# Two first layers as seven block products on one core

## The chip, the core and the metric

The kernel runs on one core of one Trainium2 chip. Times are device microseconds of one execution of the whole program. The engines are named as in the profile: PE is TensorE's matmuls, PEld its weight loads, DVE is VectorE, ACT is ScalarE, POOL is GpSimd, SP is SyncE, which issues most DMAs.

## What is computed

An attention with softmaxes over features (q) and over the sequence (k), and behind it a two-layer network with a leaky ReLU:

```python
q_s = softmax(q, axis=-1)          # q, k, v: (8, 8, 576, 64)
k_s = softmax(k, axis=2)
kv = einsum('bhsd,bhse->bhde', k_s, v)
attn = einsum('bhsd,bhde->bhse', q_s, kv)
x = attn.transpose(0, 2, 1, 3).reshape(4608, 512)
h = x @ w_in                       # w_in: (512, 2048)
g = maximum(0.01 * h, h)
out = g @ w_out                    # w_out: (2048, 512), float32 result
```

## The kernel before

Both weight matrices are kept on chip in bf16: `w_in_sb` as 4 blocks of 128 channels (`NB`) by 2048 columns, `w_out_sb` as 16 blocks of 128 rows (`NF`). The attention's result for all 4608 tokens is kept transposed, channels on the partitions, in `xT` (4 blocks by 4608, bf16). The network goes over `xT` in 9 tiles of 512 tokens (`TT`), numbered 0 to 8, the loop at L866. For each tile, the first layer (`layer1`, L560) makes 16 blocks `j` of 128 hidden units by 512 tokens, each the sum of 4 matmuls of 512 columns in one PSUM bank; `leaky` (L570) on ScalarE turns each into bf16 (`gj`, 10 buffers). The second layer (`layer2`, L582) goes over 4 subtiles of 128 tokens (`tsub`), 16 matmuls of 512 columns each; `store` (L575) copies the sum to SBUF, on ScalarE in the middle tiles and on VectorE in tile 8, and issues two DMAs on SP. The last subtile of all is split: 384 columns are copied by ScalarE, the remaining 128 by VectorE, and each part is stored by SP and ScalarE's queue side by side.

PSUM has eight banks of 512 float32 columns: six go round as `psB_pool` (first-layer blocks, attention), two as `psO_pool` (second-layer sums).

The attention of batch b (576 tokens) is made ready while earlier tiles run. The order is written out by hand: `at(t, u, ...)` (L594) hangs functions on a step of tile t, and `run(t, u)` (L599) calls them there. Steps 0 to 15 follow the first-layer blocks; steps 16 to 31 follow every fourth matmul of the second layer, so step 19 ends subtile 0 and step 23 subtile 1. For the last batch, 7, during tile 6: `q_exp` after step 2, and after step 5 `q_back`, which sums, normalizes and has `q_turn` (L547) transpose q by DMA into `qX`; at step 23 `attend_all` (L533) does the 16 matmuls of `cross` and the six copies of `x_keep` on ScalarE into `xT`. Tiles 7 and 8 have no attention beside them. The raw inputs of a batch lie in `raw_pool`, 6 buffers of 2304 float32 a partition.

Of the kernel before, what the change touches and what calls it, by code (L numbers as in the profile page):

```python
# [7 lines left out]

FP32 = mybir.dt.float32
BF16 = mybir.dt.bfloat16  # L10
AF = mybir.ActivationFunctionType
ALU = mybir.AluOpType
AX = mybir.AxisListType
# [7 lines left out]
R = 9  # L21
HL = 4
# [3 lines left out]
def kernel(  # L26
# [9 lines left out]
    nc = tc.nc  # L36
# [3 lines left out]
    B, H, S, D = q.shape  # L40
    C = H * D
    T = B * S
    Cm, F = moe_w_in.shape
    F2, O = moe_w_out.shape
    assert Cm == C and F2 == F and L * R == S and HL * 2 == H

    P = 128
    NB = C // P
    NF = F // P
    TT = 512  # L50
    NT = T // TT
    NTS = TT // P
# [2 lines left out]
    const_pool = ctx.enter_context(tc.tile_pool(name="const", bufs=1))  # L55
    w_pool = ctx.enter_context(tc.tile_pool(name="wts", bufs=1))
    xT_pool = ctx.enter_context(tc.tile_pool(name="xT", bufs=1))
    raw_pool = ctx.enter_context(tc.tile_pool(name="raw", bufs=6))
    ke_pool = ctx.enter_context(tc.tile_pool(name="ke", bufs=2))
    qe_pool = ctx.enter_context(tc.tile_pool(name="qe", bufs=2))  # L60
    mx_pool = ctx.enter_context(tc.tile_pool(name="mx", bufs=1))
    small_pool = ctx.enter_context(tc.tile_pool(name="small", bufs=3))
    qT_pool = ctx.enter_context(tc.tile_pool(name="qT", bufs=2))
    g_pool = ctx.enter_context(tc.tile_pool(name="gsb", bufs=10))
    osb_pool = ctx.enter_context(tc.tile_pool(name="osb", bufs=4))

    psB_pool = ctx.enter_context(tc.tile_pool(name="psB", bufs=6, space=bass.MemoryType.PSUM))
    psO_pool = ctx.enter_context(tc.tile_pool(name="psO", bufs=2, space=bass.MemoryType.PSUM))
    BANK_TAG = "bank2k"
# [20 lines left out]
    R7, RE = slice(0, 7), slice(7, R)  # L90
# [9 lines left out]
    nc.gpsimd.memset(zero, 0.0)  # L100
    ident = const_pool.tile([P, P], BF16)
    make_identity(nc, ident)
    identf = const_pool.tile([P, P], FP32)
    make_identity(nc, identf)
    warm = const_pool.tile([P, 1], BF16)
    nc.scalar.activation(out=warm, in_=ident[:, 0:1], func=AF.Exp)
    gate = const_pool.tile([P, 1], FP32)

    w_in_sb = w_pool.tile([P, NB, F], BF16)
    w_out_sb = w_pool.tile([P, NF, O], BF16)  # L110
    xT = xT_pool.tile([P, NB, T], BF16)


    XH, X8, XE = (slice(0, 7), slice(9, 16)), slice(7, 9), slice(16, 20)
    qe1 = const_pool.tile([P, XE.stop, P], BF16, name="qe1")
    vb2 = [const_pool.tile([P, R, 2, 2, D + 2], BF16, name=f"vb{i}") for i in range(2)]
# [85 lines left out]
    def k_exp(b, hs):  # L202
        nc.scalar.activation(  # L203
            out=st[b]["ke"][:, :, hs].rearrange("p r h d -> p h r d"),
            in_=st[b]["k"][:, hs],
            func=AF.Exp,
        )
# [36 lines left out]
    def q_first(b, rs):  # L244
# [3 lines left out]
        for gg in range(2):  # L248
# [5 lines left out]
            for h in range(2):  # L254
                for r in range(n):
                    nc.scalar.activation(
                        out=st[b]["qe"][:, rs.start + r, 2 * gg + h],
                        in_=st[b]["q"][:, 2 * gg + h, rs.start + r],
                        func=AF.Exp,
                        bias=nmax[:, 2 * gg + h, r : r + 1],  # L260
# [47 lines left out]
    def q_exp(b, rs, hs=ALLH):  # L308
        nc.scalar.activation(  # L309
            out=q_cols(b, rs, hs).rearrange("p r h d -> p h r d"),  # L310
            in_=st[b]["q"][:, hs, rs],
            func=AF.Exp,
        )
# [140 lines left out]
    def q_keep(eng, b, r0, n, gs=slice(0, 4)):  # L454
        o, i = st[b]["qT"][:, gs, r0 : r0 + n], st[b]["ps", r0][:, gs]
        if eng is nc.scalar:
            eng.copy(out=o, in_=i)
        else:
            eng.tensor_copy(out=o, in_=i)
# [65 lines left out]
    def attend_rows(b, rows, engs=(nc.scalar, nc.scalar)):  # L525
        groups = ((0, 1),) if rows.stop - rows.start <= 4 else ((0,), (1,))
        for ggs in groups:
            attend(b, ggs, rows)
        return [
            lambda ggs=ggs, hp=hp: x_keep(engs[hp], b, ggs, rows, hp) for ggs in groups for hp in range(2)  # L530
        ]

    def attend_all(b, *parts):  # L533
        for fn in sum([attend_rows(b, *p) for p in parts], []):
            fn()
# [34 lines left out]
    def leaky(o, ph):  # L570
        nc.scalar.activation(out=o, in_=ph, func=AF.Prelu, alpha=LEAKY_SLOPE)  # L571

    out_r = out.rearrange("(b l r) o -> b r l o", b=B, r=R)

    def store(row0, pout, copy=nc.vector.tensor_copy, os=slice(0, O), issue=(nc.sync, nc.sync)):  # L575
        out_sb = osb_pool.tile([P, O], FP32, name="out_sb")[:, os]
        copy(out=out_sb, in_=pout)  # L577
        for i in range(2):
            b, c = divmod(row0 + i * L, S)
            issue[i].dma_start(out=out_r[b, c // L, :, os], in_=out_sb[i * L : (i + 1) * L])  # L580

    def layer2(pout, g_sb, tsub, j, os=slice(0, O)):  # L582
        nc.tensor.matmul(  # L583
            pout,
            lhsT=g_sb[j // 2][:, j % 2, tsub * P : (tsub + 1) * P],
            rhs=w_out_sb[:, j, os],
            start=(j == 0),
            stop=(j == NF - 1),
        )
# [4 lines left out]
    def at(t, u, *fns):  # L594
        while t > 0 and u >= 32:
            t, u = t + 1, u - 32
        hooks.setdefault((t, u), []).extend(fns)

    def run(t, u):  # L599
        for fn in hooks.pop((t, u), ()):  # L600
            fn()
# [3 lines left out]
    def load_all(b, order="kqv"):  # L605
        for name in order:
            st[b][name] = load(dict(q=q, k=k, v=v)[name], b, f"{name}_raw", [(ALLH, ALLR)])
# [130 lines left out]
    def k_front(b, t, u, v, parts=(ALLH,)):  # L738
        at(t, u, lambda: k_begin(b), lambda: q_begin(b), lambda: k_tree(b, ALLH))
        at(t, v, lambda: k_allmax(b), *[lambda hs=hs: k_sub(nc.vector, b, hs) for hs in parts])  # L740

    def q_front(b, t, u):
        at(t, u, lambda: q_max(b, ALLR), lambda: q_sub(nc.vector, b, ALLR))

    def casts(b, t, u):
        at(t, u, lambda: v_cast(nc.gpsimd, b, 0), lambda: v_cast(nc.gpsimd, b, 1))

    def q_back(b, t, u):
        at(t, u, lambda: q_sum(b, ALLR), lambda: q_norm(b, ALLR), lambda: q_turn(b))
# [13 lines left out]
    for t in range(3, B - 1):  # L763
        b = t + 1
        q_front(b, t - 1, 29)
        at(t, 2, lambda b=b: q_exp(b, ALLR))
        if b + 1 < B:
            k_front(b + 1, t, 1, 8)
            casts(b + 1, t, 6)
            at(t, 17, lambda b=b: k_exp(b + 1, ALLH))  # L770
            at(t, 23, lambda b=b: attend_kv(b))
        else:
            at(t, 23, lambda b=b: attend_all(b, (R7,), (RE,)))
        q_back(b, t, 5)
        if b + 2 < B:
            at(t, 5, lambda b=b: load_all(b + 2))


    def g_tiles():
        return [g_pool.tile([P, 2, TT], BF16, name="gj") for _ in range(NF // 2)]  # L780

    g_sb = g_tiles()
# [18 lines left out]
    def end_act(j, ph, half):  # L801
# [4 lines left out]
    t2 = (  # L806
        lambda: q_transpose(0, 6, 2, psO_pool, "pout"),
        lambda: q_keep(nc.vector, 0, 6, 2),
    )
# [45 lines left out]
    pout = [psO_pool.tile([P, O], FP32, name="pout", tag="pout") for _ in range(2)]  # L855
# [7 lines left out]
    for tsub in range(NTS):  # L863
        store(tsub * P, pout[tsub])

    for t in range(1, NT):  # L866
        g_sb = []
        for j in range(NF):
            ph = psB_pool.tile([P, TT], FP32, name="ph", tag=BANK_TAG)
            layer1(j, ph, t * TT, TT)  # L870
            if j % 2 == 0:
                g_sb.append(g_pool.tile([P, 2, TT], BF16, name="gj"))
            leaky(g_sb[j // 2][:, j % 2], ph)
            run(t, j)
        for tsub in range(NTS):
            row0 = t * TT + tsub * P
            if row0 == T - P:
                for os, copy in ((slice(0, 384), nc.scalar.copy), (slice(384, O), nc.vector.tensor_copy)):
                    po = psB_pool.tile([P, os.stop - os.start], FP32, name="pout2", tag=BANK_TAG)
                    for j in range(NF):  # L880
                        layer2(po, g_sb, tsub, j, os)
                    store(row0, po, copy, os, (nc.sync, nc.scalar))
                break
            po = psO_pool.tile([P, O], FP32, name="pout", tag="pout")
            for j in range(NF):
                layer2(po, g_sb, tsub, j)
                if j == NF - 1:
                    store(row0, po, nc.scalar.copy if t < NT - 1 else nc.vector.tensor_copy)
                if j % 4 == 3:
                    run(t, 16 + 4 * tsub + j // 4)  # L890
    assert not hooks, list(hooks)


# [28 lines left out]
```

## Time and profile before

| | |
|---|---|
| Time, median of 3 runs | 281.05 us (281.03 to 281.23) |
| Span of the profiled execution | 279.3 us; its own time is not listed apart from the three, so the median stands beside it, 1.75 us longer |
| Busy share of the span | PE 97%, PEld 48%, DVE 57%, ACT 57%, POOL 18% |
| Granted TensorE clock, 183 us to the end | 1.00 of full speed |
| Longest shares of the chain that ended last | PE `pout` L583 44%, PE `ph` L562 44% |

The busy time of PE counts overlapping matmuls, whose ends are modelled; distances between starts say more. The chain of waits is followed back from the last instruction; "issue" in it is time in which nothing shows as waited for. In the groups by line the columns are: line, engine, operation, output and inputs with shapes, count, busy us, mean ns of one, idle time before and what ended it. In the timeline each row is a start, a length, engine, line and operation; rows with a count merge several. In the answers on stretches each engine has its busy time with the number of instructions, then the granted clock, the DMA share and GB/s.

### The profile page before, as it was taken

To read this page: it belongs to the slowest core of one execution; us is meant where nothing else is said; L and a number is where in the kernel's file an instruction comes from. 1 tells how busy PE (TensorE), PEld (TensorE's weight loads), DVE (VectorE), ACT (ScalarE), POOL (GpSimd) and SP (SyncE) were. 2 spreads that over 40 slices of the span, in tenths; PEclk is the share of its full clock that TensorE was granted. 3 is DMA by queue.
4 is the path that set the end of the run, shared out by engine and by line. 5 is a ranking of instruction groups with operands and counts; after the bars stand their busy time and mean duration, and the time that the engine had idled before them with its cause. 6 is when DMAs were issued, how large, how long until landed. Compare 5 with 4: busy or idle time off the path is not lost.

```text
span 279.3 us, 4849 instructions
## 1 busy us (share of the span) xinstructions
PE 272.3 (97%) x1927; PEld 133.1 (48%) x1954; DVE 158.4 (57%) x228; ACT 159.6 (57%) x283; POOL 49.5 (18%) x55
## 2 busy tenths in 40 slices
PE   8999999999999999999999999999999999999994
PEld 3488644444444454445444544454444444444443
DVE  3986986999999949957794688543700000000021
ACT  4977573783598458744675458644844464146400
POOL 2957460258003004000400140000000000000000
PEclk9999999999999999999999999999999999999999
DMA  7999999977993696099309930333033300330033
GB/s 253 326 209 325 246 242 306 403 269 200 300 410 139 116 405 227 2 307 361 78 9 311 347 77 2 84 77 75 1 87 75 75 1 2 75 75 0 2 75 75
DMA packets 40006, 46.45 MB, mean 166 GB/s; under 512 B 18736, under 2 KB 23344, under 8 KB 39984
## 3 DMA queue, kind: packets, MB, share of 16 engines
q1 hardware_dynamic: 36320, 41.82, 48.3%
q0 software_dynamic: 3504, 4.20, 8.7%
q8 instruction: 15, 0.25, 0.3%
q10 hardware_dynamic: 160, 0.13, 0.2%
q14 instruction: 7, 0.06, 0.1%
HBM read 36.70 MB, written 9.44 MB: 165 GB/s over the span
## 4 chain that ended last, share of the span: by engine, by line
PE 93%; DVE 3%; DMA 2%; issue 1%; ACT 0%; SPq 0%; ACTq 0%
PE pout L583 44%; PE ph L562 44%; DMA k_raw<-in_k_dram 2%; PE po L476 2%; DVE t L157 1%; PE pokv L338 1%; PE pkv L338 1%; PE pkv L416 0%; DVE k_raw L407 0%; ACT ke L203 0%; ACT gj L571 0%; DVE kmax L157 0%; DVE kd L431 0%; DVE kr L391 0%; PE pokv L476 0%
## 5 line engine op out<-in xcount | busy, mean ns | idle before, releaser
L583 PE MATMUL pout<-w_out_sb,gj 128*128 128x512 bf16 (+2 forms) x574 | 126.3, 373 | 1.2 <-issue 0.3
L562 PE MATMUL ph<-xT,w_in_sb 128*128 128x512 bf16 (+1 forms) x631 | 126.1, 357 | 0.5
L571 ACT ACTIVATE gj<-ph 128x512 bf16<-128x512 f32 x144 | 82.2, 601 | 26.0 <-PE ph L562 25.1
L562 PEld LDWEIGHTS <-w_in_sb 128*128 128x128 bf16 x640 | 62.3, 98 | 62.1 <-issue 0.2
L583 PEld LDWEIGHTS <-gj 128*128 128x128 bf16 x592 | 56.5, 98 | 65.6 <-issue 0.2
L577 ACT COPY out_sb<-pout 128x512 f32<-128x512 f32 (+1 forms) x29 | 16.8, 580 | 68.3 <-PE pout L583 43.1
L577 DVE COPY out_sb<-pout 128x512 f32<-128x512 f32 (+1 forms) x8 | 4.8, 637 | 70.8 <-PE pout L583 70.8
L215 POOL CAST vb<-v_raw 128x1152 bf16<-128x1152 f32 x13 | 21.1, 1650 | 81.4 <-DMA v_raw<-in_v_dram 81.4
L318 DVE TENSOR_REDUCE qsum<-qe 128x36 f32<-128x2304 bf16 (+5 forms) x13 | 20.0, 1542 | 10.5 <-ACT qe L309 10.4
L203 ACT ACTIVATE ke<-k_raw 128x2304 bf16<-128x2304 f32 (+2 forms) x13 | 18.0, 1384 | 8.4 <-DVE k_raw L195 8.0
L325 DVE TENSOR_TENSOR qe<-qe,qrec 128x2304 bf16<-128x2304 bf16 (+5 forms) x13 | 21.5, 1657 | 0.5
L242 DVE TENSOR_REDUCE qmax<-q_raw 128x36 f32<-128x2304 f32 (+5 forms) x13 | 20.0, 1539 | 0.1
L309 ACT ACTIVATE qe<-q_raw 128x2304 bf16<-128x2304 f32 (+5 forms) x13 | 17.1, 1315 | 4.3 <-POOL q_raw L301 3.4
L195 DVE TENSOR_TENSOR k_raw<-k_raw,kall 128x1152 f32<-128x1152 f32 (+2 forms) x10 | 18.0, 1820 | 0.3
L301 POOL TENSOR_TENSOR q_raw<-q_raw,qmax 128x512 f32<-128x512 f32 (+3 forms) x7 | 11.8, 1682 | 20.6 <-DMA q_raw<-in_q_dram 13.8
L499 ACT CAST xT<-po 128x448 bf16<-128x448 f32 (+3 forms) x34 | 14.4, 515 | 1.1 <-PE po L476 1.1
L301 DVE TENSOR_TENSOR q_raw<-q_raw,qmax 128x2304 f32<-128x2304 f32 (+1 forms) x6 | 14.0, 2332 | 0.2
L157 DVE TENSOR_TENSOR t<-t 128x256 f32<-128x256 f32 (+2 forms) x22 | 13.2, 599 | 0.7
L358 DVE RECIPROCAL krec<-pokv 128x2 f32<-128x2 f32 x8 | 1.3, 166 | 21.3 <-PE pokv L476 21.3
L157 DVE TENSOR_TENSOR t<-k_raw 128x512 f32<-128x512 f32 (+1 forms) x11 | 11.2, 1016 | 1.2 <-DMA k_raw<-in_k_dram 1.0
L370 PE MATMUL pout<-zero 128*128 128x512 f32 (+3 forms) x18 | 9.6, 659 | 1.0 <-POOL zero L100 1.0
L338 PEld LDWEIGHTS <-ke 64*64 64x64 bf16 x504 | 5.9, 107 | 3.4 <-issue 3.0
(68 smaller groups left out, 105.3 us busy)
## 6 DMA issues: line engine op xcount, KB each, us to landing
out_dram<-out_sb SPq DMA_DIRECT2D x70, 128.0 KB, 2.6
q_raw<-in_q_dram SPq DMA_DIRECT2D x6, 1152.0 KB, 8.8
v_raw<-in_v_dram SPq DMA_DIRECT2D x6, 1152.0 KB, 11.5
k_raw<-in_k_dram SPq DMA_DIRECT2D x5, 1152.0 KB, 6.2
k_raw<-in_k_dram SPq DMA_DIRECT2D x6, 576.0 KB, 6.1
v_raw<-in_v_dram SPq DMA_DIRECT2D x4, 576.0 KB, 7.6
w_in_sb<-in_moe_w_in_dram POOLq DMA_DIRECT2D x7, 256.0 KB, 7.0
w_out_sb<-in_moe_w_out_dram POOLq DMA_DIRECT2D x6, 256.0 KB, 9.3
```

Source lines behind the costliest of these rows:

```text
L157: nc.vector.tensor_tensor(out=o, in0=i0, in1=i1, op=ALU.max)
L195: eng.tensor_tensor(out=ks, in0=ks, in1=st[b]["kall"][:, hs].unsqueeze(2).to_broadcast([P, n, R, D]), op=ALU.subtract,)
L203: nc.scalar.activation(out=st[b]["ke"][:, :, hs].rearrange("p r h d -> p h r d"), in_=st[b]["k"][:, hs], func=AF.Exp,)
L215: eng.tensor_copy(out=o, in_=i)
L242: nc.vector.tensor_reduce(out=o, in_=st[b]["q"][:, hs, rs], axis=AX.X, op=ALU.max)
L301: eng.tensor_tensor(out=qs, in0=qs, in1=st[b]["qmax", rs.start, hs.start].unsqueeze(3).to_broadcast([P, m, n, D]), op=ALU.subtract,)
L318: nc.vector.reduce_sum(out=qsum, in_=q_cols(b, rs, hs), axis=AX.X)
L325: nc.vector.tensor_tensor(out=qes if out is None else out, in0=qes, in1=st[b]["qrec", rs.start, hs.start].unsqueeze(3).to_broadcast([P, n, ...
L562: nc.tensor.matmul(ph, lhsT=w_in_sb[:, cb, j * P : (j + 1) * P], rhs=xT[:, cb, c0 : c0 + n], start=(cb == 0 and first), stop=(cb == NB - 1 ...
L571: nc.scalar.activation(out=o, in_=ph, func=AF.Prelu, alpha=LEAKY_SLOPE)
L577: copy(out=out_sb, in_=pout)
L583: nc.tensor.matmul(pout, lhsT=g_sb[j // 2][:, j % 2, tsub * P : (tsub + 1) * P], rhs=w_out_sb[:, j, os], start=(j == 0), stop=(j == NF - 1),)
```

## The change

The first layers of tiles 7 and 8 (`TA`, `TB`) are done as one product of 2 x 2 blocks: the rows are the two tiles (`XA`, `XB`), the inner blocks two halves of the 512 channels (`CL`, `CR`), the columns two halves of the 2048 hidden units. Instead of eight block products, seven are made, from sums and differences of the blocks (the scheme of Strassen and Winograd), in groups `i` of 128 columns out of each half.

- `weight_sums` (step 12 of tile 6): four differences of weight blocks, t1 to t4, of 2 x 1024 columns each, on VectorE, and a copy b22 on GpSimd, all as float32r in five of the six `raw_pool` buffers, whose tiles are done with.
- The attention of batch 7 moves from step 23 to step 19 of tile 6.
- `token_sums` (step 22): closes the pools of the attention, opens two new ones in their place, and makes s1 to s4 on VectorE (1024 columns each) and the copy a22 on ScalarE, in float32r.
- `pair_layer1(i)`, i = 0 to 7: seven products of 2 matmuls of 512 columns, two products from the bf16 operands (`xT`, `w_in_sb`), five from the float32r sums. ScalarE copies the first (e1), VectorE combines the others in seven adds to e1 and u4 (tile 7, blocks i and 8 + i) and u3 and c22 (tile 8, the same blocks), ScalarE applies the four `leaky`. The one of u4 is held back until the next group's e1 is copied. Tile 8's blocks go into columns of `xT` that belonged to tiles 0 to 3.
- Between the products stands other TensorE work, 8 matmuls a group: in groups 0 and 1 the last subtile of tile 6, from group 2 on the second layer of tile 7, two blocks `j` a group for all four subtiles, whose sums take both `psO` banks and two of `psB`.
- At the end: the last two groups' share of tile 7's second layer (16 matmuls), its four stores with VectorE's copy, and tile 8's second layer, 4 subtiles of 16 matmuls, with ScalarE's copy and two DMAs on SP. The split of the last subtile is gone.

```diff
-    raw_pool = ctx.enter_context(tc.tile_pool(name="raw", bufs=6))
-    ke_pool = ctx.enter_context(tc.tile_pool(name="ke", bufs=2))
...
+    raw_pool = ctx.enter_context(tc.tile_pool(name="raw", bufs=6))
+    front = ctx.enter_context(ExitStack())
+    ke_pool = front.enter_context(tc.tile_pool(name="ke", bufs=2))
...
-        else:
-            at(t, 23, lambda b=b: attend_all(b, (R7,), (RE,)))
...
+    def subtract(eng, o, a, b):
+        eng.tensor_tensor(out=late[o], in0=a, in1=b, op=ALU.subtract)
+
+    def weight_sums():
+        w = lambda cs, fh: w_in_sb[:, cs, fh * (F // 2) : (fh + 1) * (F // 2)]
+        for n in ("t1", "t3", "t2", "t4", "b22"):
+            late[n] = raw_pool.tile([P, 2, R * HL * D // 2], F32R, name=n, tag="raw")[:, :, 0 : F // 2]
+        subtract(nc.vector, "t1", w(CL, 1), w(CL, 0))
+        subtract(nc.vector, "t2", w(CR, 1), plain("t1"))
+        subtract(nc.vector, "t3", w(CR, 1), w(CL, 1))
+        subtract(nc.vector, "t4", w(CR, 0), plain("t2"))
+        nc.gpsimd.tensor_copy(out=late["b22"], in_=w(CR, 1))
+
+    def token_sums():
+        front.close()
+        pool = ctx.enter_context(tc.tile_pool(name="late", bufs=1, reuse_waits="tile"))
+        late["pool"] = ctx.enter_context(tc.tile_pool(name="late2", bufs=2, reuse_waits="tile"))
...
+        nc.vector.tensor_tensor(out=late["s1"], in0=xT[:, CL, XB], in1=xT[:, CR, XB], op=ALU.add)
+        subtract(nc.vector, "s2", plain("s1"), xT[:, CL, XA])
+        subtract(nc.vector, "s3", xT[:, CL, XA], xT[:, CL, XB])
+        nc.scalar.copy(out=late["a22"], in_=xT[:, CR, XB])
+        subtract(nc.vector, "s4", xT[:, CR, XA], plain("s2"))
+
+    at(6, 12, weight_sums)
+    at(6, 19, lambda: attend_all(B - 1, (R7,), (RE,)))
+    at(6, 22, token_sums)
...
+    def product(i, w, a):
+        ps = psB_pool.tile([P, TT], FP32, name="pp", tag=BANK_TAG)
+        for c in range(2):
+            nc.tensor.matmul(ps, lhsT=w(c)[:, i * P : (i + 1) * P], rhs=a(c), start=(c == 0), stop=(c == 1))
+        return ps
+
+    def pair_layer1(i, between):
...
+        def do(w, a):
+            ps = product(i, w, a)
+            next(between)
+            return ps
+
+        nc.scalar.copy(out=e1, in_=do(wl(0), xl(0)))
+        for fn in held_leaky:
+            fn()
+        p6 = do(of("t2"), of("s2"))
+        p2 = do(wl(2), xl(2))
+        add(u2, p6, e1)
+        add(e1, p2, e1)
+        leaky(g7[i], e1)
+        add(u3, do(of("t3"), of("s3")), u2)
+        p5 = do(of("t1"), of("s1"))
+        add(u4, p5, u2)
+        add(c22, p5, u3)
+        leaky(g8(NH + i), c22)
+        add(u3, do(of("t4"), of("a22")), u3)
+        leaky(g8(i), u3)
+        add(u4, do(of("b22"), of("s4")), u4)
+        held_leaky[:] = [lambda: leaky(g7[NH + i], u4)]
...
+    def between_products():
+        for n in range(NH):
+            if n < 2:
+                todo = [lambda: next(fill, None)] * 8
+            else:
...
+                todo = [
+                    lambda tsub=tsub, j=j: pair_layer2(tsub, pouts[tsub], j)
+                    for j in (n - 2, NH + n - 2)
+                    for tsub in range(NTS)
+                ]
+            for k in range(7):
+                for fn in todo[k : k + 1 + k // 6]:
+                    fn()
+                yield
...
+    for i in range(NH):
+        pair_layer1(i, between)
+    held_leaky[0]()
+    for i in range(NH - 2, NH):
+        for j in (i, NH + i):
+            for tsub in range(NTS):
+                pair_layer2(tsub, pouts[tsub], j)
+    for tsub in range(NTS):
+        store(TA * TT + tsub * P, pouts[tsub])
+    for tsub in range(NTS):
+        po = psB_pool.tile([P, O], FP32, name="pout2", tag=BANK_TAG)
...
+        store(TB * TT + tsub * P, po, nc.scalar.copy)
```

More of the change, by code (lines that the diff above doesn't have):

```diff
@@ L10 @@
 BF16 = mybir.dt.bfloat16
+F32R = mybir.dt.float32r
 AF = mybir.ActivationFunctionType
@@ L57 @@
     xT_pool = ctx.enter_context(tc.tile_pool(name="xT", bufs=1))
-    raw_pool = ctx.enter_context(tc.tile_pool(name="raw", bufs=6))
-    ke_pool = ctx.enter_context(tc.tile_pool(name="ke", bufs=2))
[L60 to L63, printed above, removed]
     g_pool = ctx.enter_context(tc.tile_pool(name="gsb", bufs=10))
     osb_pool = ctx.enter_context(tc.tile_pool(name="osb", bufs=4))
+    raw_pool = ctx.enter_context(tc.tile_pool(name="raw", bufs=6))
+    front = ctx.enter_context(ExitStack())
+    ke_pool = front.enter_context(tc.tile_pool(name="ke", bufs=2))
+    qe_pool = front.enter_context(tc.tile_pool(name="qe", bufs=2))
+    mx_pool = front.enter_context(tc.tile_pool(name="mx", bufs=1))
+    small_pool = front.enter_context(tc.tile_pool(name="small", bufs=3))
+    qT_pool = front.enter_context(tc.tile_pool(name="qT", bufs=2))
     psB_pool = ctx.enter_context(tc.tile_pool(name="psB", bufs=6, space=bass.MemoryType.PSUM))
@@ L776, with plain @@
             at(t, 5, lambda b=b: load_all(b + 2))
+    TA, TB = NT - 2, NT - 1
+    NH = NF // 2
+    CL, CR = slice(0, 2), slice(2, 4)
+    XA, XB = slice(TA * TT, TB * TT), slice(TB * TT, NT * TT)
+    late = {}
+    def plain(n):
+        return late[n].bitcast(FP32)
+    def subtract(eng, o, a, b):
[13 more added lines that the diff above has]
+        late["pool"] = ctx.enter_context(tc.tile_pool(name="late2", bufs=2, reuse_waits="tile"))
+        both = raw_pool.tile([P, 2, R * HL * D // 2], F32R, name="s13", tag="raw")
+        for i, n in enumerate(("s1", "s3")):
+            late[n] = both[:, i, 0 : 2 * TT].rearrange("p (c n) -> p c n", c=2)
+        for n in ("s2", "s4", "a22"):
+            late[n] = pool.tile([P, 2, TT], F32R, name=n)
+        nc.vector.tensor_tensor(out=late["s1"], in0=xT[:, CL, XB], in1=xT[:, CR, XB], op=ALU.add)
[6 more added lines that the diff above has]
+    at(6, 22, token_sums)
     def g_tiles():
@@ L864, with layer2_at @@
         store(tsub * P, pout[tsub])
-    for t in range(1, NT):
+    def layer2_at(t, g, tsub, po):
+        for j in range(NF):
+            layer2(po, g, tsub, j)
+            if j == NF - 1:
+                store(t * TT + tsub * P, po, nc.scalar.copy)
+            if j % 4 == 3:
+                run(t, 16 + 4 * tsub + j // 4)
+            yield
+    for t in range(1, TA):
         g_sb = []
@@ L875 @@
         for tsub in range(NTS):
[L876 to L883, printed above, removed]
-            po = psO_pool.tile([P, O], FP32, name="pout", tag="pout")
@@ L885 @@
[L885 to L890, printed above, removed]
+            po = psO_pool.tile([P, O], FP32, name="pout", tag="pout")
+            fill = layer2_at(t, g_sb, tsub, po)
+            if (t, tsub) != (TA - 1, NTS - 1):
+                for _ in fill:
+                    pass
@@ new lines, with pair_layer2 @@
+    g7 = {}
+    g8 = lambda j: xT[:, j % NB, j // NB * TT : (j // NB + 1) * TT]
+    def pair_layer2(tsub, po, j):
+        nc.tensor.matmul(
+            po,
+            lhsT=g7[j][:, tsub * P : (tsub + 1) * P],
+            rhs=w_out_sb[:, j],
+            start=(j == 0),
+            stop=(j == NF - 1),
+        )
+    def product(i, w, a):
[3 more added lines that the diff above has]
+        return ps
@@ new lines, in pair_layer1, with add @@
+    def pair_layer1(i, between):
+        of = lambda n: (lambda c: late[n][:, c])
+        wl = lambda c0: (lambda c: w_in_sb[:, c0 + c])
+        xl = lambda c0: (lambda c: xT[:, c0 + c, XA])
+        e1, u2, u3, u4, c22 = (late["pool"].tile([P, TT], FP32, name=n) for n in ("e1", "u2", "u3", "u4", "c22"))
+        pair = g_pool.tile([P, 2, TT], BF16, name="gj")
+        g7[i], g7[NH + i] = pair[:, 0], pair[:, 1]
+        def add(o, ps, e):
+            nc.vector.tensor_tensor(out=o, in0=ps, in1=e, op=ALU.add)
+        def do(w, a):
[19 more added lines that the diff above has]
+        held_leaky[:] = [lambda: leaky(g7[NH + i], u4)]
@@ new lines @@
+    pouts, held_leaky = [], []
+    def between_products():
[3 more added lines that the diff above has]
+            else:
+                if n == 2:
+                    pouts.extend(psO_pool.tile([P, O], FP32, name="pout", tag="pout") for _ in range(2))
+                    pouts.extend(psB_pool.tile([P, O], FP32, name="pout2", tag=BANK_TAG) for _ in range(2))
+                todo = [
[6 more added lines that the diff above has]
+                    fn()
+                yield
@@ new lines @@
+    between = between_products()
+    for i in range(NH):
[9 more added lines that the diff above has]
+        po = psB_pool.tile([P, O], FP32, name="pout2", tag=BANK_TAG)
+        for j in range(NF):
+            nc.tensor.matmul(
+                po,
+                lhsT=g8(j)[:, tsub * P : (tsub + 1) * P],
+                rhs=w_out_sb[:, j],
+                start=(j == 0),
+                stop=(j == NF - 1),
+            )
+        store(TB * TT + tsub * P, po, nc.scalar.copy)
```

## The prediction

> **What bounds the kernel now.** I read the head of the page first, then its slices, then the chain of waits and the stretches of the last two token tiles.
>
> ```profile
> span 279.3 us, 4849 instructions
> PE 272.3 (97%) x1927; PEld 133.1 (48%) x1954; DVE 158.4 (57%) x228; ACT 159.6 (57%) x283; POOL 49.5 (18%) x55
> PE   8999999999999999999999999999999999999994
> DVE  3986986999999949957794688543700000000021
> ...
> 220.36 5.40 PE ph L562 x25
> ...
> 247.99 9.51 PE ph L562 x44
> ...
> 275.67 0.02 issue
> 275.69 0.29 DVE out_sb L577
> ...
> 210.00:238.00 28.00, 27.84 (x141) 12.71 (x143) 0.00 (x0) 13.90 (x26) 0.00 (x0) 1.00 0.17 38
> 238.00:266.00 28.00, 27.89 (x130) 12.67 (x130) 0.65 (x1) 11.61 (x20) 0.00 (x0) 1.00 0.17 38
> ```
>
> TensorE sets the pace: its slices are full to the end, and the chain from 220.36 (tile 7 begins) to 275.67 is nothing but matmuls at the full granted clock (1.00). That is 256 matmuls of 512 columns in 55.31 us, 0.216 us each (a tile, 220.36 to 247.99, gives the same). A matmul that goes away here is time off the span, as long as something else doesn't end later. VectorE, from 210 on, does almost nothing, and ScalarE is half idle: the change spends these two. The median of the runs is 281.05 us against a span of 279.3, so 1.75 us lie around the span; I take them as unchanged and add all differences to 281.05.
>
> **TensorE's own sum.** The two first layers have 128 matmuls. The new form has 8 groups of 7 products of 2 matmuls, 112. All else on TensorE stays (4 subtiles a tile of 16 matmuls; the last one's split in 384 and 128 columns goes, which is the same count of columns). 16 x 0.216 = **-3.46 us**, if a float32r matmul of 512 columns costs what a bf16 one does. No row shows float32r. The nearest are the float32 ones at the start:
>
> ```profile
> 9.29 0.70 PE L370 MATMUL pout<-zero 128*128 128x256 f32 x2
> 11.14 0.91 PE L370 MATMUL pout<-zero 128*128 128x384 f32 x2
> 8.21 0.33 PE L381 MATMUL kT<-identf,kmax 128*128 128x128 f32 x1
> 8.38 0.39 PE L370 MATMUL pout<-zero 128*128 128x128 f32 x2
> 8.21 0.36 PEld L370 LDWEIGHTS pout<-zero 128*128 128x128 f32 x2
> ```
>
> A plain float32 matmul is two passes (x2), and 2 x 128 more columns cost 0.91 - 0.70 = 0.21 us, so 0.82 ns a column, 0.42 us for a pass of 512. The transposing one (kT) is a single pass over four-byte data, and its successor begins 0.17 us later: a load of 128 columns (0.107 us, from 0.70 less 2 x 0.21 of columns and 0.165 of drain) and 128 columns at 0.42 ns. So four-byte data can stream at bf16's pace when one pass will do. Bounds: 0.216 us and 0.42 us a pass, or twice the latter; below bf16 nothing speaks for it. I take 0.216, by the single-pass row. The loads of the next matmul (0.36 us for two, from 8.21) run while kT is in flight, so I also take float32r's loads as hidden.
>
> **What feeds the products.** The four weight differences are 2048 columns each; a 2304-column operation takes 2.56 us, so about 2.29, 9.3 us in all. They stand behind the last row here, so VectorE has them at about 212.2. The attention of batch 7 moves one subtile earlier, to 209.1.
>
> ```profile
> 200.28 2.56 DVE L325 TENSOR_TENSOR qe<-qe,qrec 128x2304 bf16<-128x2304 bf16 x1
> 202.99 1.91 SPq L550 DMA_TRANSPOSE qX<-qe  x1
> qX<-qe SPq DMA_TRANSPOSE x1, 4.0
> 205.66 7.07 PE L583 MATMUL pout<-w_out_sb,gj 128*128 128x512 bf16 x31
> 213.30 2.40 ACT L499 CAST xT<-po 128x448 bf16<-128x448 f32 x6
> 133.11 1.22 DVE L157 TENSOR_TENSOR t<-k_raw 128x1024 f32<-128x1024 f32 x1
> L157 DVE TENSOR_TENSOR t<-k_raw 128x1024 f32<-128x1024 f32 x5 | 7.0, 1406 | 0.0
> ```
>
> Its transposed q lands at 202.99 + 4.0 = 207.0, 2 us before it is wanted (without that cover: the wait itself); no other issue on SP's queue changes its place. The six copies into xT take 2.40 us on ScalarE, moved 3.5 us up, until about 212.3. Then four token sums of 1.22 us: the second, which the second product waits for, at 214.8, the last at 217.2. TensorE starts the products at 220.2 - 3.46 = 216.7, because the last subtile of tile 6 is now filler. So the products find their operands. VectorE's first add is due 1.27 us later, 218.0, so it has 0.8 us to spare; the same 1024-column operation averages 1.41 us where GpSimd works beside it, and GpSimd copies b22 beside the weight sums, so I charge 0.2 us.
>
> **The new loop.** One group is 14 product matmuls and 8 others, 22 x 0.216 = 4.75 us on TensorE. Its results go through seven VectorE adds (u2, e1, u3, u4, c22, u3, u4) and on ScalarE the copy e1 and four leaky operations, in program order. ScalarE's order is the catch: the copy e1 of the next group stands behind the leaky of u3, which waits for the sixth add; and the next group's first add, u2, waits for that copy. That is a ring. Its links:
>
> ```profile
> L577 DVE COPY out_sb<-pout 128x512 f32<-128x512 f32 x7 | 4.6, 686 | 68.0 <-PE pout L583 68.0
> L157 DVE TENSOR_TENSOR t<-k_raw 128x512 f32<-128x512 f32 x6 | 4.1, 691 | 1.2 <-DMA k_raw<-in_k_dram 1.0
> 9.77 0.75 DVE L407 TENSOR_TENSOR k_raw<-k_raw,kallp 128x576 f32<-128x576 f32 x1
> 10.74 0.70 DVE L407 TENSOR_TENSOR k_raw<-k_raw,kallp 128x576 f32<-128x576 f32 x1
> 46.27 1.88 DVE L577 COPY out_sb<-pout 128x512 f32<-128x512 f32 x3
> 134.37 1.51 DVE L157 TENSOR_TENSOR t<-t 128x512 f32<-128x512 f32 x1
> L309 ACT ACTIVATE qe<-q_raw 128x512 bf16<-128x512 f32 x3 | 1.9, 627 | 0.9 <-POOL q_raw L301 0.9
> L577 ACT COPY out_sb<-pout 128x512 f32<-128x512 f32 x28 | 16.3, 584 | 55.8 <-PE pout L583 30.7 <-issue 16.6 <-DMA out_dram<-out_sb 8.6
> 195.13 2.12 ACT L309 ACTIVATE qe<-q_raw 128x2304 bf16<-128x2304 f32 x1
> 197.15 0.59 ACT L571 ACTIVATE gj<-ph 128x512 bf16<-128x512 f32 x1
> 197.28 2.55 DVE L318 TENSOR_REDUCE qsum<-qe 128x36 f32<-128x2304 bf16 x1 [6.28 <-ACT qe L309]
> ```
>
> An add from PSUM and SBUF of 512 columns: the copy and the SBUF form say 0.69, the 576-column form with a PSUM operand (0.70 and 0.75), less 64 columns, 0.64 to 0.68. I take 0.68. Three operations that need nothing of each other take 1.88, (1.88 - 0.68)/2 = 0.60 from start to start; one that waits for the one before starts 0.035 after its end (133.11 + 1.22 to 134.37), so 0.715. In the instructions the second and the sixth add wait for their forerunner (both overwrite what it read), the third and fourth don't, and the fifth waits for the third, which is over by then: first to sixth 2 x 0.715 + 3 x 0.60 = 3.23. Then 0.68 for the sixth, 0.03 to ScalarE (as 195.13 + 2.12 to 197.28), 0.53 until the next operation there may start (0.627, less the 0.10 by which 197.15 overlaps 195.13 + 2.12), 0.584 for the copy, 0.03 back: 1.85. The ring takes **5.08 us**, 0.33 more than TensorE needs. Banks don't bind: with two of six held by tile 7's sums four remain, and each product's bank is released at least half a us before the ring needs that product.
>
> Counted from the first product: first add at 1.27; seven rings 35.56; 0.48 once, as ScalarE copies out tile 6's last subtile inside the ring of group 2 (0.584 less the overlap); sixth add of the last group 3.23 later at 40.55, the seventh from 41.15 to 41.83, leaky of u4 0.63 and twice 0.03 of release: 42.5, plus the 0.2 from above, 42.7. That value is wanted by the matmuls of j=15, before which TensorE has 8 x 22 + 8 + 4 = 188 matmuls, 40.6 us. So TensorE loses **+2.1 us**, mostly in bits of 0.3 a group.
>
> **The end.** The last subtile was copied out in two parts, the second by VectorE while two queues stood ready; now ScalarE copies 512 columns, then SP issues both stores.
>
> ```profile
> 276.01 0.47 SPq L580 DMA_DIRECT2D out_dram<-out_sb  x1
> out_dram<-out_sb SPq DMA_DIRECT2D x2, 128.0 KB, 2.3
> out_dram<-out_sb ACTq DMA_DIRECT2D x1, 32.0 KB, 2.1
> ```
>
> Copy 0.584 for 0.29, the second issue 0.47 or a little more behind the first, landing 2.3 for 2.1: **+1.0 us**. Tile 7's four copies and stores lie under tile 8's 64 matmuls (13.8 us).
>
> Sum: -3.46 + 2.1 + 1.0 = -0.36, so 281.05 becomes 280.7 us.
>
> **Rules of the notes.** The rows show an unwaited VectorE operation starting before the last one's end, and a waiting one 0.035 after it. The Trainium skill, "VectorE: DVE Perf Modes", section on the DRAIN you can't avoid, says a next operation can't start until the pipe is empty and that semaphores then cost nothing extra. By that all adds would be 0.715 apart, which is the third rival; the trace speaks against it (1.88 for three), and the page itself exempts operations that aren't held. The Trainium skill, "TensorE: Matmul & The Clock Gate", section on weight-path perf modes, says the fast weight load is off for FP32. The trace agrees in so far as a four-byte load works out at 0.107 us; whether float32r's is hidden no run here shows. That is the second rival.
>
> **Rivals.**
> 1. The adds are shorter and the ring doesn't bind. At 0.64 it takes 2 x 0.675 + 3 x 0.56 + 0.64 + 1.17 = 4.84, and the last value arrives as TensorE wants it: -3.46 + 1.0, 278.6 us. For it: the 0.70 row. Against: 686 and 691. Chance 0.09.
> 2. Slower: float32r's weight load lies in the open, because the matmul carries it and can't send it ahead. 80 matmuls x 0.107 = 8.6 us, which takes in the ring's 2.1: -3.46 + 8.6 + 1.0, 287.2 us. It decides from 0.031 us a matmul on ((3.46 - 1.0)/80). For it: separate load instructions are issued for bf16 only. Against: loads under kT. Chance 0.10.
> 3. Slower: every add waits for a full drain. First to sixth 3.58, ring 5.43; over seven rings and the last group 2.9 us more than forecast, 283.6 us. Chance 0.04.
> 4. The sums don't run as one full-rate pass: 0.42 a matmul, 80 x 0.204 = 16.3 us, 294.9 us; two passes, far more. So the change wouldn't save what it says. Against: kT. Chance 0.06.
>
> **How the numbers follow.** The forecast (ring binds) has 0.71. Its own range is 279.5 (add 0.66, ring 4.96) to 282 (add 0.70, ring 5.20, a later first add). About 0.2%, 0.56 us, is what a measurement can tell from no change; the forecast lies inside it, and 0.01 us an add moves it by 0.5 us. Of the 0.71 I give faster 0.31, same 0.26, slower 0.14. With rival 1 faster is 0.40; same 0.26; with rivals 2, 3 and 4 slower 0.34. The range leaves out rivals 2 to 4 (0.20) and reaches down to rival 1: 278.4 to 282.8.
>
> **What would show it.** Right: first adds of successive groups about 5.1 us apart, VectorE's idle time in front of u2 released by ScalarE's copy, TensorE's gaps in the groups at the banks of products and about 2 us in sum; float32r matmuls 0.216 apart where they don't wait; the final copy 0.58 long. Wrong: groups 4.75 apart with VectorE waiting for TensorE (rival 1); full TensorE slices with product matmuls over 0.25 apart (2, 4); adds 0.72 apart throughout (3).

## The result, and the profile after

The changed kernel takes 282.14 us (median of 5 runs) against 281.23 for the kernel before in the same comparison: a ratio of 1.0037, 95% interval 1.0024 to 1.0049, so 0.9 us slower. The forecast was 280.7 us, 0.13% under the 281.05 it started from; the time lies in its range, on the other side.

The head of the page and its slices:

```profile
span 280.4 us, 4875 instructions
PE 270.9 (97%) x1895; PEld 134.3 (48%) x1922; DVE 208.8 (74%) x292; ACT 164.4 (59%) x291; POOL 50.4 (18%) x56
PE   8899999999999999999999999999999989999993
DVE  3986986999999959948793779452898788888400
```

VectorE, empty in these slices before, is now busy seven to eight tenths of the time from 217 us to 259; TensorE's tenths hardly change. That isn't enough to see who waits. The chain that ended last (start, length, what) tells it; the pieces are those around the groups and the end:

```profile
238.99 0.57 ACT e L967
239.59 0.70 DVE u L960
240.38 0.69 DVE e L960
241.08 1.19 DVE u L960 x2
242.27 0.61 DVE c L960
242.97 0.70 DVE u L960
243.72 0.52 issue
244.24 0.58 ACT e L967
...
260.07 0.61 ACT gj L573
260.73 1.04 PE pout L937 x4
...
275.62 0.59 ACT out_sb L579
```

Where this chain before was TensorE alone, it now goes round one figure: copy e1 on ScalarE, five adds, the sixth, the leaky of u3 (shown as "issue", 0.52), the copy e1 again. From 239.59 to 244.84 one turn is 5.25 us. And the last leaky, of u4, releases the four matmuls of j=15 at 260.73. The copy of the last subtile starts at 275.62. In the answer on waits (engine and line, waited for, us in total, times, longest) for 205 us to the end, the first add of a group stands behind that copy:

```profile
DVE u L960 <- ACT e L967: 5.6, 8, 1.1
PEld pp L948 <- DVE c L960: 1.0, 3, 0.4
PEld pp L948 <- DVE u L960: 0.8, 3, 0.3
PE pout L937 <- ACT out_sb L579: 0.6, 1, 0.6
```

TensorE's own waits are few in this list, since a matmul that runs late still overlaps its neighbours; the distances in the timeline show them.

### The profile page after: what moved, and what is told of

It reads as the page before. It is cut to its first block, busy times and chain, and to the rows that moved or that the text cites. A ratio compares the mean times of both kernels' runs of the same rounds, so it can differ in the third digit from the quotient of the medians.

```text
span 280.4 us, 4875 instructions
## 1 busy us (share of the span) xinstructions
PE 270.9 (97%) x1895; PEld 134.3 (48%) x1922; DVE 208.8 (74%) x292; ACT 164.4 (59%) x291; POOL 50.4 (18%) x56
## 4 chain that ended last, share of the span: by engine, by line
PE 83%; DVE 9%; ACT 2%; issue 2%; DMA 2%; SPq 0%; DVEq 0%
PE pout L585 35%; PE ph L564 34%; PE pout L1018 5%; DVE u L960 4%; PE pp L948 4%; DMA k_raw<-in_k_dram 2%; PE po L478 2%; PE pout L937 1%; DVE e L960 1%; DVE c L960 1%; DVE t L159 1%; PE pokv L340 1%; ACT e L967 1%; PE pkv L340 1%; PE pkv L418 0%
## 5 line engine op out<-in xcount | busy, mean ns | idle before, releaser
L585 PE MATMUL pout<-w_out_sb,gj 128*128 128x512 bf16 x432 | 100.6, 379 | 1.1 <-issue 0.3
L564 PE MATMUL ph<-xT,w_in_sb 128*128 128x512 bf16 (+1 forms) x505 | 98.3, 352 | 0.4
L573 ACT ACTIVATE gj<-ph 128x512 bf16<-128x512 f32 x112 | 63.2, 603 | 17.6 <-PE ph L564 16.7
L564 PEld LDWEIGHTS <-w_in_sb 128*128 128x128 bf16 x512 | 49.8, 98 | 47.0 <-DMA w_in_sb<-in_moe_w_in_dram 0.3
L585 PEld LDWEIGHTS <-gj 128*128 128x128 bf16 x448 | 42.8, 98 | 52.4 <-issue 2.9
L579 ACT COPY out_sb<-pout 128x512 f32<-128x512 f32 x28 | 16.3, 583 | 52.7 <-PE pout L585 19.4
L217 POOL CAST vb<-v_raw 128x1152 bf16<-128x1152 f32 x13 | 20.1, 1577 | 83.7 <-DMA v_raw<-in_v_dram 67.8
L960 DVE TENSOR_TENSOR u<-pp,u 128x512 f32<-128x512 f32 x32 | 20.6, 684 | 0.8
L937 PE MATMUL pout<-w_out_sb,gj 128*128 128x512 bf16 x62 | 20.4, 384 | 0.7 <-ACT out_sb L579 0.6
L948 PE MATMUL pp<-s,t 128*128 128x512 f32 x48 | 18.2, 479 | 0.0
L1018 PE MATMUL pout<-w_out_sb,xT 128*128 128x512 bf16 x62 | 13.9, 379 | 0.1
```

Of the source, the lines that this page charges most:

```text
L564: nc.tensor.matmul(ph, lhsT=w_in_sb[:, cb, j * P : (j + 1) * P], rhs=xT[:, cb, c0 : c0 + n], start=(cb == 0 and first), stop=(cb == NB - 1 ...
L585: nc.tensor.matmul(pout, lhsT=g_sb[j // 2][:, j % 2, tsub * P : (tsub + 1) * P], rhs=w_out_sb[:, j, os], start=(j == 0), stop=(j == NF - 1),)
L937: nc.tensor.matmul(po, lhsT=g7[j][:, tsub * P : (tsub + 1) * P], rhs=w_out_sb[:, j], start=(j == 0), stop=(j == NF - 1),)
L948: nc.tensor.matmul(ps, lhsT=w(c)[:, i * P : (i + 1) * P], rhs=a(c), start=(c == 0), stop=(c == 1))
L960: nc.vector.tensor_tensor(out=o, in0=ps, in1=e, op=ALU.add)
L1018: nc.tensor.matmul(po, lhsT=g8(j)[:, tsub * P : (tsub + 1) * P], rhs=w_out_sb[:, j], start=(j == 0), stop=(j == NF - 1),)
```

## The experiments

Two theories were set against each other. A: the ring through ScalarE's program order sets the pace, 5.25 us a group. B: TensorE is late by itself, since float32r matmuls cost more, and the ring only happens to be as long. The kernel before was timed beside each, with medians from 281.10 to 281.44; differences below are to the kernel before of the same comparison, so that 282.14 stands as +0.91.

**Held leaky of u3.** 

> The leaky of u3 is held back behind the next group's copy e1, as the one of u4 already is; nothing else changes. Theory A (the ring of adds, leaky of u3 and copy e1 sets the pace, 5.25 us a group in the changed kernel): the first adds of successive groups come 4.99 us apart, which is TensorE's own pace in group 0, and the matmuls of j=15 start about 1.3 us earlier: 280.8 us. Theory B (TensorE itself is late, by float32r matmuls that cost more than bf16 ones; the ring only happens to be about as long): no change, 282.1 us.

```diff
-        leaky(g8(i), u3)
...
-        held_leaky[:] = [lambda: leaky(g7[NH + i], u4)]
+        held_leaky[:] = [lambda: leaky(g8(i), u3), lambda: leaky(g7[NH + i], u4)]
...
-    held_leaky[0]()
+    for fn in held_leaky:
+        fn()
```

280.58 us, ratio 0.9982 (0.9974 to 0.9991), -0.52, so 1.4 less than the change. VectorE's timeline, the first adds of groups 3 and 4:

```profile
233.13 0.69 DVE L960 TENSOR_TENSOR u<-pp,e 128x512 f32<-128x512 f32 x1 [0.31 <-PE pp L948]
238.11 0.69 DVE L960 TENSOR_TENSOR u<-pp,e 128x512 f32<-128x512 f32 x1 [0.30 <-PE pp L948]
```

And the waits of the same kernel from 216 us on:

```profile
DVE u L960 <- PE pp L948: 1.9, 6, 0.3
DVE u L960 <- ACT e L967: 1.4, 2, 1.1
```

Six of the eight first adds now wait for TensorE, and they come 4.98 us apart, TensorE's own pace. With one leaky moved in the order, and no work less, the pace passed from the ring to TensorE: theory A.

**Longer ring, and the same work beside it.** 

> ScalarE makes one more copy of 512 columns (u3 to a tile that nobody reads) right behind the leaky of u3, that is inside the ring. Theory A: every ring is about 0.54 us longer, 5.8 us, and the last leaky too: +4.3 us, 286.4 us. Theory B: ScalarE has room (busy 70% in the groups), TensorE sets the pace: +0.5 us at most, 282.6 us.

```diff
         leaky(g8(i), u3)
+        nc.scalar.copy(out=late["pool"].tile([P, TT], FP32, name="xtra"), in_=u3)
```

286.73 us, ratio 1.02 (1.0185 to 1.0215), +5.6 (two runs near 286.2 and two near 287.2), so 4.7 more than the change; groups come 5.77 apart. 

> The same extra copy of u3 on ScalarE as in the longer ring, but behind the next group's copy e1 and the leaky of u4, where ScalarE waits about 1.0 us for the add e1 in every group: beside the ring. Theory A: ring 5.25 us, time as the changed kernel, 282.1 us, within 0.3. If it is ScalarE's work as such that costs (0.54 us a group), +4 us as in the longer ring, 286.5 us.

```diff
-        held_leaky[:] = [lambda: leaky(g7[NH + i], u4)]
+        xtra = late["pool"].tile([P, TT], FP32, name="xtra")
+        held_leaky[:] = [lambda: leaky(g7[NH + i], u4), lambda: nc.scalar.copy(out=xtra, in_=u3)]
```

282.35 us, ratio 1.0036 (1.0022 to 1.0049), +1.1: as the change, with groups 5.25 apart. ScalarE does the same work in both; its place in the order alone makes about 4.5 us.

**Sums in bf16.** 

> All ten sums and copies are kept in bf16 instead of float32r, so the result is rounded more coarsely; order and counts of work stay. Theory A: the ring stays at 5.25 us a group, TensorE only waits longer in it: 282.1 us, within 0.3. Theory B: 80 float32r matmuls at 0.024 us more each than bf16 (group 0 takes 4.99 us where 22 bf16 matmuls take 4.75) go away, 1.9 us: 280.2 us.

```diff
-F32R = mybir.dt.float32r
+F32R = mybir.dt.bfloat16
```

(with the sizes and views of these tiles to match). 282.23 us, ratio 1.0040 (1.0028 to 1.0053): as the change, against theory B. In TensorE's timeline group 0 runs without waits in both kernels. The first product of groups 0 and 1, first in the changed kernel, then with bf16 sums:

```profile
216.74 0.59 PE L948 MATMUL pp<-xT,w_in_sb 128*128 128x512 bf16 x2
221.73 0.59 PE L948 MATMUL pp<-xT,w_in_sb 128*128 128x512 bf16 x2
```

```profile
216.68 0.59 PE L948 MATMUL pp<-xT,w_in_sb 128*128 128x512 bf16 x2
221.42 0.59 PE L948 MATMUL pp<-xT,w_in_sb 128*128 128x512 bf16 x2
```

4.99 against 4.74 us: ten float32r matmuls cost 0.25 us more than ten bf16 ones. Float32r does cost, but behind a ring of 5.25 us it can't be seen in the time.

**Split last subtile.** 

> The last subtile of tile 8 gets back its split in 384 columns (copied by ScalarE) and 128 (copied by VectorE), each stored by SP and ScalarE's queue side by side; nothing else changes. From the two spans behind the start of the last copy, 3.61 us before and 4.78 after: -1.1 us, 281.0 us. If the end of the span hangs on something else (the other stores, the kernel's closing), no change, 282.1 us. Theories A and B don't differ here.

```diff
-        store(TB * TT + tsub * P, po, nc.scalar.copy)
+            store(TB * TT + tsub * P, po, copy, os, (nc.sync, nc.scalar if tsub == NTS - 1 else nc.sync))
```

(for the last subtile with `os` and `copy` as in the kernel before). 281.01 us, ratio 0.9998 (0.9989 to 1.0007), so 1.0 less than the change.

**No overwriting.** 

> The second and the sixth add write tiles of their own instead of overwriting what the add before them reads, so neither waits for its forerunner; ScalarE's order is that of the changed kernel. Theory A, with the prediction's error in the waiting adds (0.78 us from start to start in the trace, against 0.715): both become 0.61, the ring 5.25 - 2 x 0.17 = 4.91 us, under TensorE's 4.99, so the groups come 4.99 apart: 280.6 us, as with the held leaky. If the 0.78 has another cause than the wait (two operands of which one was just written): no change, 282.1 us.

(e2 and u5 are new tiles)

```diff
-        add(e1, p2, e1)
-        leaky(g7[i], e1)
+        add(e2, p2, e1)
+        leaky(g7[i], e2)
...
-        add(u3, do(of("t4"), of("a22")), u3)
-        leaky(g8(i), u3)
+        add(u5, do(of("t4"), of("a22")), u3)
+        leaky(g8(i), u5)
```

281.10 us, ratio 0.9993 (0.9984 to 1.0002), 1.1 less than the change where 1.5 was expected; the groups come 4.85 to 5.05 us apart but for two of 5.28 and 5.47; in the longest the copy of tile 6's last subtile lies in the ring. So the ring can also be shortened on VectorE's side, and the waits of the two adds are what was too long.

**Wait taken ahead.** 

> In the changed kernel's order, VectorE copies one column of the product ahead of the second and of the sixth add. That small copy takes over the wait for TensorE, so these two adds wait for VectorE alone. Asked is why they start 0.78 us behind the add before them (0.10 after its end) where a waiting operation of the kernel before started 0.04 after: the profile has three separate semaphore instructions a group on VectorE, just for the adds with two waits. If the two waits are the reason: the adds start 0.03 to 0.05 after the end of the one before, 0.73 us apart, ring 5.15 us, about -0.8 us in time. If it is the overwriting of an operand that is still being read: 0.78 as before, 282.1 us. If the small copies cost more than they save: over 0.78 apart, slower.

```diff
+        look(p2)            # tensor_copy of one column
         add(e1, p2, e1)
...
-        add(u3, do(of("t4"), of("a22")), u3)
+        p4 = do(of("t4"), of("a22"))
+        look(p4)
+        add(u3, p4, u3)
```

281.23 us, ratio 0.9997 (0.9987 to 1.0006), 1.1 less than the change, with 16 VectorE operations more. VectorE's timeline in group 4 of this kernel, and behind it the same place in the changed kernel:

```profile
239.03 0.69 DVE L960 TENSOR_TENSOR u<-pp,e 128x512 f32<-128x512 f32 x1 [0.57 <-ACT e L970]
239.64 0.15 DVE L963 COPY look<-pp 128x1 f32<-128x1 f32 x1
239.76 0.69 DVE L960 TENSOR_TENSOR e<-pp,e 128x512 f32<-128x512 f32 x1
...
244.14 0.69 DVE L960 TENSOR_TENSOR u<-pp,e 128x512 f32<-128x512 f32 x1 [0.57 <-ACT e L970]
```

```profile
239.59 0.69 DVE L960 TENSOR_TENSOR u<-pp,e 128x512 f32<-128x512 f32 x1 [0.57 <-ACT e L967]
240.38 0.69 DVE L960 TENSOR_TENSOR e<-pp,e 128x512 f32<-128x512 f32 x1
```

In the answer on the adds' line, VectorE's separate semaphore instructions (count, shortest/median/longest ns, first and last start), here and in the changed kernel:

```profile
L960 DVEq EVENT_SEMAPHORE  x9: 21/21/3256, 214.7 to 253.4; - x9
```

```profile
L960 DVEq EVENT_SEMAPHORE  x24: 21/21/3251, 214.8 to 258.7; - x24
```

The second add starts 0.73 us after the first instead of 0.79, although an operation stands between them, and the ring is 5.11 us instead of 5.25. The overwriting is the same in both kernels, so the long link comes from the way in which the second wait is taken. The trace's records name the semaphore of each wait. In the changed kernel the second and the sixth add carry the wait for TensorE themselves, and the one for VectorE, which is the late one, stands in the separate semaphore instruction ahead of them; they start 0.10 us after their forerunner's end. Here the small copy has the wait for TensorE, the adds carry the one for VectorE themselves, and they start 0.035 us after that end.

Two waits alone don't make a link long. The first add of a group has two as well, the one for ScalarE in the instruction itself, and starts 0.03 us after the copy's end (239.56 to 239.59 in the chain). The trace of the kernel before has both cases too:

```profile
26.84 0.75 DVE L157 TENSOR_TENSOR t<-t 128x256 f32<-128x256 f32 x2
27.70 0.29 DVE L157 TENSOR_TENSOR kmax<-t,k_raw 128x128 f32<-128x128 f32 x1
```

```profile
142.03 0.38 DVE L320 RECIPROCAL qrec<-qsum 128x36 f32<-128x36 f32 x1
142.44 2.56 DVE L325 TENSOR_TENSOR qe<-qe,qrec 128x2304 bf16<-128x2304 bf16 x1
```

The second operation of each pair has two waits. At 27.70 the wait for the forerunner is the separate one, and 0.10 us pass from its end; at 142.44 the operation carries that wait itself, and 0.035 us pass. The one at 56.58 is like the first; eight others are like the second.

**Held leaky and split.** 

> Held leaky of u3 and split last subtile together. The two effects lie in different places (groups; last copy and store), so they should add: -1.6 and -1.1 from 282.14, 279.5 us, 0.55% below the kernel before. If the earlier end of the groups only moves a wait to the last stores, about 280.5 us.

279.89 us, ratio 0.9951 (0.9938 to 0.9963), -1.4 to the kernel before and 2.3 to the change; expected were 2.6. The two effects add up, nearly.

**The same with bf16 sums.** 

> As the one with held leaky and split, with all sums in bf16 (coarser rounding of the result). With the ring out of the way TensorE is paced by its own matmuls, so the 0.025 us that a float32r matmul takes more must now show: groups 4.75 us apart instead of 4.99, 8 x 0.24 = 1.9 us less, 277.6 us. If VectorE's seven adds (0.78 + 0.61 + 0.60 + 0.61 + 0.78 + 0.61 + 0.61 = 4.60 us) or the banks bind first: between 277.6 and 279.5 us.

277.84 us, ratio 0.9882 (0.9869 to 0.9896), -3.4. With the ring gone, float32r's surplus shows in full: 2.05 us between the last two. This is the fastest version; its sums are rounded to bf16.

**Products together.** 

> Held leaky and split as before, but the 8 other matmuls of a group stand behind its seven products instead of between them, so in group 0 eight float32r matmuls follow each other without a bf16 one. Asked is the distance of their starts there. If a float32r matmul takes 0.024 us more each: 0.240 us throughout. If the surplus is paid where TensorE changes from bf16 to float32r (five times a group, about 0.05 us each): 0.216 within the row. In time this order is worse in either case: products come faster than VectorE's adds (0.43 to 0.48 us against 0.61 to 0.78), banks run out and TensorE waits; over 281 us.

```diff
-                for fn in todo[k : k + 1 + k // 6]:
+                for fn in todo if k == 6 else ():
```

280.63 us, ratio 0.9972 (0.9960 to 0.9983): slower than the interleaved order by 0.7 us, and not over 281 as expected, since VectorE nearly kept up; the groups come 4.9 apart at first and 5.16 from group 3 on. TensorE's timeline in group 0, from the fourth product's matmuls on:

```profile
218.05 1.28 PE L948 MATMUL pp<-s,t 128*128 128x512 f32 x4
219.17 0.62 PE L948 MATMUL pp<-a,t 128*128 128x512 f32 x2
219.62 0.62 PE L948 MATMUL pp<-s,b 128*128 128x512 f32 x2
220.09 1.90 PE L585 MATMUL pout<-w_out_sb,gj 128*128 128x512 bf16 x8
```

From 219.17 to 220.09 lie four distances from a float32r matmul to the next start, 0.230 us each; from 218.47, the start of the second one in the row of four as a narrower window shows it, there are seven of 0.231. That is neither 0.240 nor 0.216. About 0.015 us belong to the matmul itself; of the 0.25 in an interleaved group that is 0.15, and the remaining 0.1 presumably goes with the changes between the two types; no run took those alone.

## Why the prediction was wrong

**What feeds the products** held. The products start at 216.74 (forecast 216.7); the sums are ready in time, the first add starts at 218.11 (218.0).

**TensorE's own sum** was right in the count and off in the price: a group takes 4.99 us, not 4.75, 0.025 more for each float32r matmul. It cost nothing in the changed kernel (bf16 sums changed nothing) and 2.05 us as soon as the ring was broken. That this error, 2 us of the forecast saving, didn't show in the time is luck: the ring is the longer of the two. Rival 2, the load in the open at 0.107 us (0.115 by the figures that the prediction subtracts), didn't come, nor did rival 4, 0.42 us a matmul. The Trainium skill, "TensorE: Matmul & The Clock Gate", section on weight-path perf modes, says that FP32 gains nothing from the fast weight load; the trace agrees in so far as the four-byte float32r loads show 190 ns beside 98 for bf16. They run under the matmul before; the surplus of a float32r matmul, 0.015 us in a row and 0.025 between bf16 ones, is the most that can be left of them.

**The new loop** was the right mechanism: a ring through ScalarE's order, TensorE waiting in every group. Held leaky, longer ring and the same work beside it show the mechanism. What failed is the size of one link, the step "one that waits for the one before starts 0.035 after its end, so 0.715". The second and the sixth add start 0.10 after it, 0.78 to 0.80 us behind the start of the one before. The row that gave 0.035 was of an operation with one wait; these two wait for VectorE and for TensorE, and the wait for VectorE stands in a separate instruction. A row with that arrangement (27.70) stood in the trace of the kernel before. With the wait for TensorE taken ahead, the link is 0.73 and the ring 5.11, the forecast's 5.08 but for 0.03. The other links hold: adds of 0.68 to 0.69 (so rival 1, shorter adds, didn't come), unwaited ones 0.60 to 0.61 apart (so rival 3, a full drain behind each, didn't come), and 1.87 from the sixth add to the next group's first (forecast 1.85). Seven rings at 0.17 more are 1.2 us, and the two long links of the last group add 0.15: the matmuls of j=15 began at 260.73, 43.99 us after the first product, instead of 42.7, and less the 40.6 us of matmuls TensorE lost 3.39 us instead of 2.1.

**The end** cost 1.17 us by the spans behind the start of the last copy (4.78 against 3.61), 1.0 by the kernel with the split; forecast 1.0.

The sum becomes -3.46 + 3.39 + 1.17 = +1.10 us; the span grew by 1.1, the median by 0.9. The change saves 3.46 us of matmuls by count, and in the changed kernel nearly all of that is lost behind the ring. ScalarE's order isn't the whole price, though: held leaky wins back 1.4 us, and then float32r's own surplus sets the pace. The ring, the surplus and the lost split had all to go before the full 3.4 us showed. With the split alone brought back, the change is level with the kernel before (281.01 us). The time lies just above the forecast's own range (279.5 to 282) and inside the wider one only by its upper 0.8 us, for which the prediction names no term. The forecast's own sensitivity (0.01 us an add is half a us) had been worked out, but the start behind a separate wait was not among the values that it varied.

## What to carry to other kernels

When an engine off the critical path gets work in a loop, follow one value round all engines in program order: an operation that nobody needs soon, standing in front of one that the next turn waits for, joins the turns into a ring, and its length, not any engine's busy share, is the pace. Here moving one leaky behind one copy was worth 1.4 us, and doing the same work beside the ring instead of in it about 4.5 us. Price each link by a row whose late wait is taken in the same way, by the operation itself or by a separate instruction ahead of it, and bring a dropped detail of the end back before judging a change by its time.

## What of the hardware had not been expected

- On VectorE, an operation that carried the wait for its forerunner itself started about 0.035 us after that one's end, with or without a second, earlier wait; where a separate semaphore instruction took that wait, it started 0.09 to 0.105 us after it. An added small copy that made the operation carry it again made the kernel faster by about 1.1 us.
- Float32r matmuls of 512 columns in a row start 0.231 us apart, bf16 ones 0.216; mixed with bf16 ones, each costs 0.025 us more.
